# A routed mixture-of-experts kernel: the last sum of h ahead of the next expert's weight sums, and a buffer of its own for the odd group's outputs

## The chip, the cores and the metric

The kernel runs on one core of one Trainium2 chip. The metric is device time in microseconds of one execution, lower is better. Before the change three executions took 673.17, 674.33 and 680.16 us; the median is 674.33.

## What is computed

Two blocks follow each other. The first is attention within chunks of 64 tokens, for 8 batches, 8 heads and 576 tokens each. Its output, 4608 tokens by 512 channels, goes through a router with eight experts: each token takes the expert whose embedding is nearest by cosine, is sent through that expert's two weight matrices with a ReLU between, and is scaled by its gate. All is float32.

```python
logits = xn @ en.T / tau
expert_idx = np.argmax(logits, axis=1)
probs = np.exp(logits - logits.max(-1, keepdims=True)); probs /= probs.sum(-1, keepdims=True) + 1e-09
gate_w = probs[np.arange(N), expert_idx]
for e in range(E):                       # E = 8, N = 4608, D = 512, F = 1024
    mask = expert_idx == e
    h = np.maximum(x[mask] @ w1[e], 0.0)
    out[mask] = gate_w[mask, None] * (h @ w2[e])
```

## The kernel before

**The two halves.** In the first half, up to about 190 us, the kernel computes attention and the routing, and writes every token to a place in a table in DRAM that is sorted by expert. In the second half it takes the tokens in groups. A group is two lanes of 64 tokens, and each lane has its own expert: lane 0 starts at the first expert and goes up, lane 1 starts at the last and goes down. So a lane changes its expert now and then, while the other goes on with its own. Which groups change is known only at run time; the flags lie in a tile `swap`.

**A step.** The main loop over `j` computes the hidden layer of group `j + 1` in `hidden_fast`, then the second product of group `j` in `result`. Both are matmuls on TensorE (PE), at L342 and L413. `hidden_fast` saves multiplications in the manner of Strassen and Winograd: `x @ w1` is made of seven products of half-sized blocks, named p1 to p7 in the code. They are issued in the order p1, p2, p3, p5, p6, p7, p4. Some of them use blocks of `w1` itself (B11, B21, B22), the others sums of blocks: T1, T2 and T4 lie in the tile `sums`, T3 lies in the place of B12 within `w1`. The sums are made on VectorE (DVE) by `add_up` (L291). They depend on the expert alone, so they are made again only when a lane changes its expert.

Each of the seven products goes to a PSUM bank. Six banks rotate (`bank`), so a product must wait until the product issued six before it has been read. p4 waits for p1 of the same group, which is read by a copy on ScalarE (ACT, L377). p7 waits for p4 of the group before, which is read by the last sum of h.

**From products to h.** DVE adds the products into four quarters of h (L374: c11, c12, c22 and, last, U minus p4). After each quarter ACT applies the ReLU (L361, two instructions of 64 rows). When both quarters of a half of h are there, `turn` transposes that half on DVE (L368): `turn(0)` for the first, `turn(1)` for the second. The result `hT` is what L413 of the next step multiplies with `w2`.

**Around it.** `turn_next` transposes the inputs of the group after (L203), makes the sums of its inputs (L318, tile S) and issues further loads on the queue of SyncE (SP). The gate of that group is worked out a bit at a time between these (L224 to L234; its square root and its exponential each need a table load on ACT). `swap_next` calls `take_next` (L295 on): for each lane it loads the flag from `swap` into a register on DVE and on GpSimd (POOL), and branches. Only if the lane changes its expert, POOL copies three blocks of the new weights from `next_w1` over the old ones (L301), and DVE runs the four sums of `add_up`.

**The order.** The kernel gives the order by hand: each engine runs its instructions in the order of the code, and waits for others through semaphores. So what stands where in `hidden_fast` decides what is queued behind what on DVE and ACT.

**The outputs.** `result` scales the second product by the gate on ACT (L421) into a buffer `y`, of which there is one, and POOL scatters its rows to the output (L428). The group numbered `LEAST` may be a single lane (one lane has an odd group left over); then its outputs are 128 rows of 256, and it is handled in `step_alone` at the end, right behind `result` of the last pair (`before_last`).

Of the kernel before, what the change touches and what calls it, by code (L numbers as in the profile page):

```python
# [9 lines left out]
FP32 = mybir.dt.float32  # L10
# [8 lines left out]
P = 128  # L19
# [6 lines left out]
def kernel(  # L26
# [12 lines left out]
    B, H, S, Dh = q.shape  # L39
    E, D = moe_expert_emb.shape  # L40
# [3 lines left out]
    KD = D // P  # L44
# [4 lines left out]
    Q = 32  # L49
# [13 lines left out]
    def buf_of(j):  # L63
        return 0 if j < LONE else (j - LONE + 1) % 2
# [54 lines left out]
    bp = ctx.enter_context(tc.tile_pool(name="blk", bufs=2))  # L119
# [156 lines left out]
    def block(s, m, w1=None):  # L276

        if m in TS:
            return sums_sb[s][:, TS.index(m)]
        u, v = UV[m]  # L280
        return (w1 or w1_sb)[s].rearrange("p (u c) (v x) -> p u v c x", u=2, v=2)[:, u, v]
# [13 lines left out]
    def take_next(j):  # L295

        for s in range(2):
            f = number(swap[of_step(s, j)], 1, ENG.DVE, ENG.Pool)
            with tc.If(f > 0):  # L299
                for m in ("B11", "B21", "B22"):  # L300
                    nc.gpsimd.tensor_copy(block(s, m), block(s, m, next_w1))  # L301
                add_up(s, next_w1, ("T1", "T2", "T3", "T4"))

    def quarters(xT):
        return xT.rearrange("p (u c) (s b i) -> p u b c s i", u=2, s=2, b=2)
# [17 lines left out]
    def bank(ps_h, shape):  # L323
        tag = f"h{bank_no[0] % 6}"
        bank_no[0] += 1
        return ps_h.tile(shape, FP32, tag=tag, name=tag)

    def hidden_fast(j, ps_h, gate, turn_next, swap_next):

        d = mo[j]  # L330
        x = quarters(d["xT"])
        s1, s2, s3, s4 = d["S"]
        W2 = KF * Q

        def product(a, m):
            ps = bank(ps_h, [P, W2])
            for c in range(KD // 2):
                for s in range(2):
                    w = block(s, m)[:, c].rearrange("p (r x) -> p r x", r=2)
                    for r in range(2):  # L340
                        t0 = G * s + Q * r
                        nc.tensor.matmul(  # L342
                            ps[t0 : t0 + Q],
                            lhsT=a[:, c, s],
                            rhs=w[:, r],
                            start=c == 0,
                            stop=c == KD // 2 - 1,
                        )
            return ps


        last = "_last" if j == LEAST - 1 else ""
        hT = bp.tile([P, KF, P], FP32, tag="hT" + last, name="hT", bufs=1 if last else 2)
        d["hT"] = hT
        C = late_p.tile([P, 4, W2], FP32, tag="C", name="C")
        U, c11, c12, c22 = (C[:, i] for i in range(4))
        h = [late_p.tile([P, 2, W2], FP32, tag=f"h{b}", name=f"h{b}") for b in range(2)]

        def relu(b, v, x):
            for s in range(2):  # L360
                nc.scalar.activation(  # L361
                    h[b][G * v : G * v + G, s].rearrange("p (k i) -> p k i", i=Q),
                    x[G * s : G * s + G].rearrange("p (i k) -> p k i", i=Q),
                    AF.Relu,
                )

        def turn(b):
            nc.vector.transpose(  # L368
                hT.rearrange("p k (s b i) -> p b s k i", b=2, i=Q)[:, b],
                h[b].rearrange("p s (k i) -> p s k i", i=Q),  # L370
            )

        def add(out, a, b, op=ALU.add):
            nc.vector.tensor_tensor(out, a, b, op)  # L374

        p1 = product(x[:, 0, 0], "B11")
        nc.scalar.copy(U, p1)  # L377
        next(gate, None)
        next(gate, None)
        p2 = product(x[:, 1, 0], "B21")  # L380
        add(c11, U, p2)
        next(gate, None)
        relu(0, 0, c11)
        turn_next()
        p3 = product(s4, "B22")
        p5 = product(s1, "T1")
        p6 = product(s2, "T2")
        add(U, U, p6)
        add(c12, U, p5)
        add(c12, c12, p3)  # L390
        relu(0, 1, c12)
        for _ in gate:
            pass
        p7 = product(s3, "T3")
        add(U, U, p7)
        add(c22, U, p5)
        relu(1, 1, c22)
        p4 = product(x[:, 1, 1], "T4")
        swap_next()
        add(U, U, p4, ALU.subtract)  # L400
        relu(1, 0, U)
        turn(0)
        turn(1)

    def result(j, ps_y):
        d = mo.pop(j)
        ps = ps_y.tile([P, D], FP32, tag="y", name="y_ps")
        one_group = j == LEAST
        w = D // 2 if one_group else D
        for c in range(KF):  # L410
            for r in range(P // Q):
                t0, s, d0 = (r % 2, 0, w * (r // 2)) if one_group else (r, r // 2, 0)
                nc.tensor.matmul(  # L413
                    ps[Q * r : Q * r + Q, 0:w],
                    lhsT=d["hT"][:, c, Q * t0 : Q * t0 + Q],
                    rhs=w2_sb[s][buf_of(j)][:, c, d0 : d0 + w],
                    start=(c == 0),
                    stop=(c == KF - 1),
                )
        y = bp.tile([P, D], FP32, tag="y", name="y", bufs=1)  # L420
        nc.scalar.activation(y[:, 0:w], ps[:, 0:w], AF.Copy, scale=gate_of.pop(j))  # L421
        to, at, bound = out, spot[:, j % SPOTS, TOK : TOK + 1].bitcast(I32), N - 1
        if one_group:

            at2 = bp.tile([P, 1], I32, tag="at2", name="at2")
            nc.vector.tensor_scalar(at2, at, 2.0, second, ALU.mult, ALU.add)
            to, at, bound = out.rearrange("n (s d) -> (n s) d", s=2), at2, 2 * N - 1
        ins = nc.gpsimd.indirect_dma_start(  # L428
            out=to,
            out_offset=bass.IndirectOffsetOnAxis(ap=at, axis=0),  # L430
            in_=y[:, 0:w],
            in_offset=None,
            bounds_check=bound,
            oob_is_err=False,
        )
        tc.declare_no_dep(ins.ins, group="rows", reason="blocks hold different tokens")
        tc.add_to_no_dep_group("rows", ins.ins)
# [8 lines left out]
    with (  # L446
# [590 lines left out]
        for t in range(-3, NT + 3):  # L1037
# [24 lines left out]
            if 0 <= t < NT:  # L1062
                values(t)
                b = (2 * t + 2) // NCB + 1
# [43 lines left out]
    late_p = ctx.enter_context(tc.tile_pool(name="late", bufs=1, reuse_waits="tile"))  # L1108
# [11 lines left out]
    with (  # L1120
# [18 lines left out]
        for j in range(LEAST - 1):  # L1139
            n = j + 2  # L1140

            def turn_next():
                if n < LEAST:
                    turn_xb(n)
                    if n + XBUF < NJ:
                        load_x(n + XBUF)
                    add_x(n)

            def swap_next():
                if NE <= n < LEAST:  # L1150
                    take_next(n)

            if j == 0:
                first_parts()
                add_up(0, None, TS)
                first_parts()
            elif j == 1:
                turn_next()
                add_up(1, None, TS)
                hidden_plain(2, w1_sb, lambda s: add_up(s, None, ("T3",)))  # L1160
            else:
                gate = gate_parts(n) if n < LEAST else iter(())
                hidden_fast(j + 1, ps_h, gate, turn_next, swap_next)

            result(j, ps_y)
            if NE <= next_of(j) < NJ:
                load_w2(next_of(j))
# [9 lines left out]
        def before_last():  # L1177
            result(LEAST - 1, ps_y)
            load_w2(LEAST + 1)

        def step_alone(j, between=None):
            turn_xb(j)
            if j + XBUF < NJ:
                load_x(j + XBUF)
            gates(j)
            hidden_plain(j, next_w1)
            if j + 1 < NJ:
                load_late(j + 1)
            if between is not None:
                between()  # L1190
            result(j, ps_y)
            if j + 2 < NJ:
                load_w2(j + 2)
# [51 lines left out]
```

## Time and profile before

| | |
|---|---|
| median of three executions | 674.33 us |
| the profiled execution | 673.4 us |
| its span, first to last instruction | 671.6 us |
| share of the span busy: PE / DVE / ACT / POOL | 93% / 63% / 64% / 26% |
| mean granted TensorE clock | 0.978 |
| DVE, sums of w1 for a new expert (L291, from `next_w1`) | 6 changes of 4 sums, 1.22 us each |
| DVE, sums of h (L374) | 231, 0.416 us each; idle before them 49.8 us |
| DVE, `turn` (L368) | 66, 0.708 us each |
| ACT, ReLU (L361) | 264, 0.678 us each; idle before them 101.8 us |
| ACT, y (L421) | 37, 0.682 us each |

A row gives the time an engine was at work on such instructions, and the idle time that came just before them. Idle time of an engine that isn't the bound costs nothing by itself. An arrow in brackets, as in `[1.54 <-DVE C L374]`, names what ended that idle time: the engine, the tile and the line. An engine name with a q (DVEq) is its sequencer, which handles register loads, branches and waits. `x16` is the number of instructions merged into one row; their time is from the first's start to the last's end.

### The profile page before, as it was taken

Reading aid. Unit: us, or ns where it says so; the run is one execution under the profiler, and the core shown is the slowest. Engines: PE = TensorE matmul, PEld = TensorE weight load, DVE = VectorE, ACT = ScalarE, POOL = GpSimd, SP = SyncE. Lnnn points to the kernel's source line nnn. Section 1 sums busy time; section 2 is a strip of 40 time slices with the busy share of each in tenths; the row PEclk is TensorE's granted clock in tenths of the full one; section 3 lists DMA queues with packets and bytes.
Section 4 is the critical chain, followed back from the end, with each engine's and each line's share of the span. In section 5 each row is a group of like instructions: output and inputs, shape, how many; then the busy total and the mean of one; then the engine's idle time right before and its main releaser. Section 6 shows DMA issues by size and latency. Waiting matters only on the chain. (4 is left out here: it accounts for less than half of the span.)

```text
span 671.6 us, 24878 instructions
## 1 busy us (share of the span) xinstructions
PE 626.3 (93%) x9744; PEld 343.6 (51%) x9744; DVE 425.9 (63%) x1140; ACT 427.7 (64%) x758; POOL 175.2 (26%) x255
## 2 busy tenths in 40 slices
PE   4988999999899979999999999988999999999993
PEld 3867888786343436555434444433444444444441
DVE  2858888886498535656576566768565667565430
ACT  4656677675225837674867877565877766867740
POOL 6648887843320101002110102202101020100101
PEclk9889899999899979999999999999999999999998
DMA  9898899989818711112787111776821114511101
GB/s 246 221 267 232 245 290 289 278 247 367 316 45 300 294 34 46 44 39 61 286 313 254 54 36 47 283 283 227 325 77 37 50 44 164 175 43 34 50 26 39
DMA packets 94687, 112.67 MB, mean 168 GB/s; under 512 B 52460, under 2 KB 72684, under 8 KB 94552
## 3 DMA queue, kind: packets, MB, share of 16 engines
q1 hardware_dynamic: 82824, 72.84, 34.0%
q0 software_dynamic: 11696, 38.04, 17.1%
q8 instruction: 81, 1.33, 0.8%
q14 instruction: 54, 0.44, 0.2%
q10 hardware_dynamic: 32, 0.02, 0.0%
HBM read 334.71 MB, written 22.69 MB: 532 GB/s over the span
## 5 line engine op out<-in xcount | busy, mean ns | idle before, releaser
L413 PE MATMUL y_ps<-w,hT 128*32 128x512 f32 (+1 forms) x2368 | 265.4, 591 | 3.6 <-DMA w<-in_moe_w_dram 3.6
L361 ACT ACTIVATE h<-C 64x256 f32<-64x256 f32 x264 | 179.0, 678 | 101.8 <-DVE C L374 99.4
L413 PEld LDWEIGHTS y_ps<-w,hT 128*32 128x32 f32 x2368 | 84.1, 111 | 160.0 <-issue 147.6
L428 POOL DMA_INDIRECT out_dram<-y,spot x36 | 35.1, 975 | 414.9 <-ACT y L421 238.7
L374 DVE TENSOR_TENSOR C<-C,h 128x256 f32<-128x256 f32 x231 | 96.1, 416 | 49.8 <-DVEq L299 39.2
L342 PE MATMUL h<-sums,xbT 128*32 128x256 f32 x1056 | 81.0, 380 | 5.0 <-DVEq L299 2.6
L342 PE MATMUL h<-w,S 128*32 128x256 f32 x1056 | 81.4, 379 | 3.2 <-DVE w L291 1.7
L342 PE MATMUL h<-w,xbT 128*32 128x256 f32 x1056 | 68.5, 379 | 0.0
L368 DVE STREAM_TRANSPOSE hT<-h 128x512 f32<-128x512 f32 x66 | 46.7, 708 | 28.2 <-ACT h L361 28.1
L227 DVE TENSOR_SCALAR rn<-rn 128x1 f32<-128x1 f32 x37 | 5.7, 153 | 82.3 <-ACT rn L224 82.3
L342 PEld LDWEIGHTS h<-w,xbT 128*32 128x32 f32 x1056 | 37.7, 110 | 34.1 <-issue 17.0
L342 PEld LDWEIGHTS h<-sums,xbT 128*32 128x32 f32 x1056 | 38.5, 110 | 28.8 <-ACT C L377 4.3
L342 PEld LDWEIGHTS h<-w,S 128*32 128x32 f32 x1056 | 39.1, 110 | 26.0 <-DVE C L374 2.0
L421 ACT ACTIVATE y<-y_ps,gate 128x512 f32<-128x512 f32 (+1 forms) x37 | 25.2, 682 | 37.5 <-issue 25.9
L813 POOL DMA_INDIRECT spots<-xr,dest x36 | 37.4, 1038 | 30.3 <-DVE dest L778 9.8
L203 DVE STREAM_TRANSPOSE xbT<-xin 128x256 f32<-128x256 f32 x73 | 44.5, 649 | 0.5 <-DVE hT L368 0.5
L224 ACT ACT_TABLE_LOAD x34 | 43.6, 1283 | 0.9 <-issue 0.4
L231 ACT ACT_TABLE_LOAD x34 | 43.6, 1283 | 0.6
L342 PE MATMUL h<-sums,S 128*32 128x256 f32 x528 | 40.9, 379 | 0.0
L695 ACT COPY xT<-tr 128x512 f32<-128x512 f32 x36 | 21.1, 585 | 29.9 <-PE tr L693 29.9
L585 POOL DMA_DIRECT2D kx<-in_k_dram x36 | 32.0, 891 | 19.1 <-PE tr L608 18.3
L585 POOL DMA_DIRECT2D qx<-in_q_dram x40 | 34.5, 866 | 0.3 <-PE tr L608 0.2
(202 smaller groups left out, 801.6 us busy)
## 6 DMA issues: line engine op xcount, KB each, us to landing
w<-in_moe_w_dram SPq DMA_DIRECT2D x74, 2048.0 KB
next_w<-in_moe_w_dram SPq DMA_DIRECT2D x67, 2048.0 KB
xin<-spots SPq DMA_DIRECT2D x158, 64.0 KB
qx<-in_q_dram POOLq DMA_DIRECT2D x32, 256.0 KB
v<-in_v_dram SPq DMA_DIRECT2D x56, 144.0 KB
kx<-in_k_dram POOLq DMA_DIRECT2D x28, 256.0 KB
spots<-blank SPq DMA_DIRECT2D x9, 144.0 KB
spot<-spots SPq DMA_DIRECT2D x80, 4.0 KB
```

Source lines behind the costliest of these rows:

```text
L203: nc.vector.transpose(xT[:, :, cols].rearrange("p c (b i) -> p b c i", i=Q), t[:, s * (D // 2) : (s + 1) * (D // 2)].rearrange("p (b i c) ...
L224: nc.scalar.activation(rn, spot[:, j % SPOTS, SQ : SQ + 1], AF.Sqrt)
L231: nc.scalar.activation(sh, sh, AF.Exp, accum_out=gate)
L342: nc.tensor.matmul(ps[t0 : t0 + Q], lhsT=a[:, c, s], rhs=w[:, r], start=c == 0, stop=c == KD // 2 - 1,)
L361: nc.scalar.activation(h[b][G * v : G * v + G, s].rearrange("p (k i) -> p k i", i=Q), x[G * s : G * s + G].rearrange("p (i k) -> p k i", i=Q),
L368: nc.vector.transpose(hT.rearrange("p k (s b i) -> p b s k i", b=2, i=Q)[:, b], h[b].rearrange("p s (k i) -> p s k i", i=Q),)
L374: nc.vector.tensor_tensor(out, a, b, op)
L413: nc.tensor.matmul(ps[Q * r : Q * r + Q, 0:w], lhsT=d["hT"][:, c, Q * t0 : Q * t0 + Q], rhs=w2_sb[s][buf_of(j)][:, c, d0 : d0 + w], start= ...
L421: nc.scalar.activation(y[:, 0:w], ps[:, 0:w], AF.Copy, scale=gate_of.pop(j))
L428: ins = nc.gpsimd.indirect_dma_start(out=to, out_offset=bass.IndirectOffsetOnAxis(ap=at, axis=0), in_=y[:, 0:w], in_offset=None, bounds_ch ...
L585: eng.dma_start(out=x[done : done + n], in_=src[b, :, s : s + n, :].rearrange("h p d -> p h d"),)
L813: ins = nc.gpsimd.indirect_dma_start(out=spots, out_offset=bass.IndirectOffsetOnAxis(ap=at, axis=0), in_=m, in_offset=None, bounds_check=S ...
```

## The change

There are two edits. In `hidden_fast` the call of `swap_next()` moves from ahead of the last sum of h to a place between `turn(0)` and `turn(1)`. So on DVE the last sum (U minus p4) and `turn(0)`, and on ACT the ReLU of that sum, are issued before the flags are loaded and, where an expert changes, before the four sums of the next w1. In `result` the odd group takes a buffer of the tile S (two of them, used for the sums of inputs in the main loop) in place of the common `y`.

```diff
@@ hidden_fast
         p4 = product(x[:, 1, 1], "T4")
-        swap_next()
         add(U, U, p4, ALU.subtract)
         relu(1, 0, U)
         turn(0)
+        swap_next()
         turn(1)
@@ result
-        y = bp.tile([P, D], FP32, tag="y", name="y", bufs=1)
+        if one_group:
+            S = late_p.tile([P, 3, KD // 2, 2, Q], FP32, tag="S", name="S", bufs=2)
+            y = S.rearrange("p a c b i -> p (a c b i)")
+        else:
+            y = bp.tile([P, D], FP32, tag="y", name="y", bufs=1)
         nc.scalar.activation(y[:, 0:w], ps[:, 0:w], AF.Copy, scale=gate_of.pop(j))
```

## The prediction

> **What bounds the kernel now.** I read the busy table first: TensorE (PE) is busy for 93% of the span, no other engine for more than 64%. So the end can only move if PE's idle time, or work after PE's last matmul, moves. The chain of waits does not help here: it runs back through POOL's own queue. Next I cut the routed half into steps, from the first matmul of one group's second product (`result`, L413) to the first of the next, and asked for the busy time in six of them.
>
> ```profile
> PE 626.3 (93%) x9744; PEld 343.6 (51%) x9744; DVE 425.9 (63%) x1140; ACT 427.7 (64%) x758; POOL 175.2 (26%) x255
> ```
>
> ```profile
> 401.55:414.45 12.90, 12.90 (x180) 5.72 (x176) 7.23 (x20) 9.46 (x15) 3.98 (x4) 1.00 0.14 43
> 414.45:427.37 12.92, 12.92 (x181) 5.72 (x177) 9.61 (x19) 6.53 (x10) 1.11 (x2) 1.00 0.45 149
> 307.72:322.31 14.59, 13.89 (x188) 7.60 (x186) 10.77 (x21) 6.96 (x11) 2.15 (x3) 1.00 0.43 145
> 335.22:349.90 14.68, 13.72 (x180) 5.72 (x176) 11.92 (x23) 8.07 (x14) 3.20 (x4) 1.00 0.80 297
> 427.37:443.56 16.19, 13.35 (x180) 5.58 (x176) 12.34 (x25) 8.80 (x14) 3.80 (x4) 1.00 0.88 331
> 456.47:472.21 15.74, 13.73 (x181) 5.72 (x177) 12.98 (x23) 8.09 (x14) 2.60 (x3) 1.00 0.73 264
> ```
>
> After the window come its length, then PE's busy time. An undisturbed step lasts 12.9 and PE never rests in it. Six steps hold a change of w1 (sums at 313.9, 341.2, 418.1, 435.2, 463.5 and 553.3; call them S1 to S6). S3 (second line) and S6 still last 12.9. S1, S2, S4 and S5 are the last four lines: 1.7, 1.8, 3.3 and 2.8 too long, **9.6 us in all**. That is what this part of the change can win. (The steps starting at 240.5 and before are lengthened by a w2 load, 3.60 us of PE idle; nothing here touches that.)
>
> The timeline of VectorE (DVE), ScalarE (ACT) and PE in S4 shows the cause:
>
> ```profile
> 432.79 0.86 DVE L374 TENSOR_TENSOR C<-C,h 128x256 f32<-128x256 f32 x2
> 435.16 1.23 DVE L291 TENSOR_TENSOR sums<-next_w 128x1024 f32<-128x1024 f32 x1 [1.52 <-DVEq L299]
> ...
> 439.84 0.41 DVE L374 TENSOR_TENSOR C<-C,h 128x256 f32<-128x256 f32 x1
> 440.17 0.70 DVE L368 STREAM_TRANSPOSE hT<-h 128x512 f32<-128x512 f32 x1
> ```
>
> ```profile
> 440.28 1.36 ACT L361 ACTIVATE h<-C 64x256 f32<-64x256 f32 x2 [4.88 <-DVE C L374]
> 441.67 0.69 ACT L421 ACTIVATE y<-y_ps,gate 128x512 f32<-128x512 f32 x1
> 442.26 0.36 ACT L377 COPY C<-h 128x256 f32<-128x256 f32 x1
> ```
>
> ```profile
> 440.30 1.07 PE L342 MATMUL h<-w,S 128*32 128x256 f32 x16 [1.54 <-DVE C L374]
> 442.67 1.07 PE L342 MATMUL h<-sums,xbT 128*32 128x256 f32 x16 [1.30 <-ACT C L377]
> ```
>
> The last sum of h (439.84) stands behind the four sums of w1; ACT idles 4.88 for it, and the y and the copy of the next group's p1 stand behind its ReLU. PE waits twice for a PSUM bank: until that last sum has read p4 (1.54), then until the copy has read p1 (1.30).
>
> **What the Trainium skill says.** "PSUM — Partial Sum Buffer" (Engine vs sequencer instructions): ScalarE, VectorE and GpSimd run strictly first in, first out. The trace agrees: y and copy follow the ReLU at once, though y's matmuls ended by 434.4. "GPSIMD Engine Reference" (Specifications): GpSimd shares its SBUF interfaces with VectorE. It agrees: beside POOL's weight copies (411.4 to 414.4) the add of S at L318 took 0.54, elsewhere 0.29. "DMA: Bandwidth & Descriptors" (Anatomy of one DMA) puts a fixed 2.0 us on a transfer, mostly the write's receipt. It agrees: the last full y was handed over by 659.48 and its buffer came free about 661.6, 2.1 later.
>
> **Part 1: the moved sums.** No instruction is added or removed. Per step the block moved on DVE is two register loads and branches (skipped if the expert stays) and, for a changed lane, four sums of 1.22. It moves behind one add (0.42) and `turn(0)` (0.70). POOL's part (three copies of 1.03) is in the same block, but nothing else of POOL lies between, and its copies start when p3 frees them, before DVE gets there. The block issues no DMA and no SP work lies between; the next w1 load, which waits for the sums' reading, starts under 1 us later, and a lane's next change is at least 45 us away.
>
> *How much later the sums start.* In S3 the last c22 add starts at 417.36 and the sums at 418.06, 0.70 later: register load and branch. After: the moved add waits for c22's end (417.84), `turn(0)` follows 0.33 later (440.17 after 439.84), and needs the ReLU of c12, which ends at 418.15. So `turn(0)` at 418.2, sums at 418.9: **0.84 later**.
>
> *What that may cost.* Lane 1's first product with T1 waits for the whole of lane 0's block: PE restarted in S2 and S5 only after lane 0's fourth sum. In S3 that block ended at 422.88 and PE loaded T1's weights at 423.70. 422.88 + 0.84 + 0.05 = 423.77, a stall of 0.07. So S3 and S6 lose about 0.1 each.
>
> *What it gives.* The last sum and its ReLU no longer wait for the w1 sums, so both bank waits end early. In S4 (lane 1, no block of lane 0 ahead) each sum is also ready before its product. I follow the start of the last c22 add, relative to the step's start: 2.9 in S3. Register load to `turn(1)` then takes 6.5 for lane 0 and 7.6 for lane 1; the chain from `turn(1)` to the next last c22 add, with the ReLU and gate no longer late, is 0.7 + 5.3 (562.62 to 567.92), so the next step's value is x + 12.5 − 12.9 or x + 13.6 − 12.9. In a quiet step it falls by 12.91 − 11.35: ACT repeats every 11.55 when it is behind (copies at 560.71 and 572.26), of which only the 0.20 idle before the last ReLU goes. It stops at 2.4 (2.9 beside POOL's copies).
> - S1: x = 4.2. T1 is ready before PE wants it; the copy of p1 is in time. No stall.
> - S2: from S1, 4.9, then 3.3, plus about 0.7 beside POOL: 4.1 instead of 5.3. The lane-0 block ends at 4.1 + 0.84 + 5.52 + 0.05 = 10.5 after the start; PE wants it at 9.25. Stall 1.25.
> - S4: from S3, 2.9 − 0.4, plus 0.5: 3.0 instead of 5.9. No stall: **3.3** won.
> - S5: back at 2.9; stall 0.1: **2.7** won.
>
> S1 and S2 belong together: until S1's stall PE's column groups run about 0.8 apart (matmuls of two products alternate, `result` lasts 7.83 instead of 7.05), and the stall that aligns them costs that too. So S1 and S2, 3.45 before, keep about 1.35: **2.1** won. Sum: 2.1 + 3.3 + 2.7 − 0.2 = **7.9**. Bounds: 9.6, and about 5 if S2 gains nothing and each lane-0 change stalls by 0.3.
>
> *What hides the rest.* In quiet steps the register loads (1.5) move under the last ReLU, which `turn(1)` waits for anyway; DVE is idle there. That cover is 1.4 to 1.5 long, and if it goes, `turn(1)` has until the next `result`.
>
> **Part 2: the odd group's outputs.** One buffer was shared:
>
> ```profile
> 661.68 0.47 ACT L421 ACTIVATE y<-y_ps,gate 128x256 f32<-128x256 f32 x1 [3.45 <-DMA out_dram<-y,spot]
> 662.43 0.99 POOL L428 DMA_INDIRECT out_dram<-y,at  x1 [2.95 <-ACTq L1199]
> ```
>
> PE's last matmul ends at 660.86, so the eviction can start 0.75 earlier, and the scatter with it. In a buffer of S, free for many steps, no new wait arises: in the built program this eviction waits for PE and DVE alone. But SP's last load issue ends at 662.86, and the span at 671.6. Whether those 8 us follow POOL or SP the page does not show: gain 0 to 0.8; I take **0.4**.
>
> **Sum.** 7.9 + 0.4 = 8.3. The profiled execution took 673.4, so 665.1. The median of the runs shown is 674.33, 0.9 higher: **666.0**. About 1% (6.7 us, so 667.6) is what can be told from no change.
>
> **Rivals.**
> *Lag stays (0.23).* ACT is busy 9.5 of 12.9 in a step; if DVE's chain behind the sums does not shorten, S2 and S5 keep their waits and pay 0.84 each, S3 and S6 0.1 each. S1 (1.7) and S4 (3.3) still win. 5.0 − 1.9 + 0.4 = 3.5: 670.8. Against it: DVE's rn sits idle 1.73 for ACT after each such ReLU, which goes.
> *Slower (0.05).* `turn(0)` stands ahead of the sums and waits for ACT. If the ReLU of c12 comes late (it ended only 0.05 before it would be wanted), the delay d grows from 0.84, and every lane-0 change pays: S2 and S5 d each, S3 and S6 d − 0.8. With S1 and S4's 5.0 and the 0.4, it decides from 2d + 2(d − 0.8) = 5.4, d = 1.75. At d = 2.5 the kernel takes 677.
> *It does nothing (0.04).* PE's waits are replaced by one for w2: those loads, 4.2 MB, land 14.4 after `result` ends (329.96 after 315.55) and are wanted 18.8 after it. 4.4 are left, so I exclude nearly all of this: 674.3. That the order is not what the text says is excluded: DVE's built order has the add and `turn(0)` ahead of the loads in every step.
>
> **Numbers.** Forecast 0.68: 663.5 to 668. The range adds most of the first rival: 663.2 to 670.2. Faster by over 1%: 0.68 (nearly all of the forecast, little else); slower by over 1%: 0.03; the rest 0.29.
>
> **What would show it.** Right: no idle of PE before L342 put down to ACT C L377 or DVE C L374; S4's step near 12.9; S3 and S6 at most 13.1; S2 about 14; ACT's idle before its ReLU down from 99.4; the last eviction within 0.1 of PE's end. Wrong: lane-0 steps of 13.5 or more in S3, S5 and S6 (the delay is larger than 0.84), or S4 still above 14.5 (the lag stays).

## The result, and the profile after

The change makes the kernel faster, by about what was forecast. Over 14 executions each the medians are 668.01 us after and 676.60 before, a ratio of 0.987 with a 95% interval of 0.9838 to 0.9902. That is 8.6 us less (6.6 to 11.0 by the interval); 8.3 had been forecast. 668.01 lies within 663.2 to 670.2, at the upper edge of the 663.5 to 668 to which the forecast gave most of its chance; it is 2.0 above the 666.0 because this time the kernel before itself had a median 2.3 higher than the 674.33 that the forecast started from.

The profiled execution after took 667.17, with a span of 665.4 (before: 673.4 and 671.6). From its page, the busy table's first entries and the groups that answer to those of before:

```profile
PE 624.7 (94%) x9744; PEld 390.1 (59%) x9744; DVE 427.0 (64%) x1140; ACT 430.3 (65%) x758; POOL 180.7 (27%) x255
...
L361 ACT ACTIVATE h<-C 64x256 f32<-64x256 f32 x264 | 178.9, 678 | 71.7 <-DVE C L374 68.9
...
L374 DVE TENSOR_TENSOR C<-C,h 128x256 f32<-128x256 f32 x231 | 96.0, 416 | 11.2 <-PE h L342 4.4
L342 PE MATMUL h<-sums,xbT 128*32 128x256 f32 x1056 | 96.1, 379 | 0.6 <-DVEq L299 0.6
...
L368 DVE STREAM_TRANSPOSE hT<-h 128x512 f32<-128x512 f32 x66 | 46.7, 708 | 55.0 <-ACT h L361 54.2
```

No engine runs more or fewer instructions. ACT's idle time ahead of the ReLU fell from 101.8 to 71.7, and DVE's idle time ahead of the sums of h from 49.8 to 11.2, while that ahead of `turn` rose from 28.2 to 55.0: most of it only changed its place. The column to read is PE's. In the whole routed half PE idles 0.6 us for `hidden_fast`, in one place, where it idled 8.2 before (3.2 ahead of `h<-w,S` and 5.0 ahead of `h<-sums,xbT`).

The six steps with a change of w1, in the windows of the trace after (length, PE's busy time, then PE's weight loads, DVE, ACT, POOL):

```profile
310.62:323.53 12.91, 12.91 (x184) 8.45 (x180) 11.59 (x23) 8.21 (x14) 2.87 (x3) 1.00 0.33 100
336.44:349.35 12.91, 12.91 (x184) 8.45 (x180) 12.11 (x27) 9.77 (x16) 4.65 (x4) 1.00 0.69 238
...
413.89:426.81 12.92, 12.92 (x184) 8.46 (x180) 12.19 (x26) 9.49 (x16) 2.71 (x3) 1.00 0.43 139
426.81:439.71 12.90, 12.90 (x183) 8.44 (x179) 11.59 (x23) 8.09 (x12) 3.40 (x4) 1.00 0.84 305
...
452.62:466.50 13.88, 13.32 (x183) 7.35 (x179) 13.22 (x27) 10.26 (x17) 5.92 (x4) 1.00 0.58 198
543.96:557.07 13.11, 13.11 (x182) 5.68 (x178) 12.45 (x27) 10.13 (x17) 1.14 (x1) 1.00 0.44 144
```

S1 to S4 are undisturbed. S5 keeps 0.97 and S6 has 0.20 that it did not have before.

DVE and ACT in S4, the step that was 3.28 too long. First DVE:

```profile
430.89 1.38 DVE L374 TENSOR_TENSOR C<-C,h 128x256 f32<-128x256 f32 x3
432.18 0.70 DVE L368 STREAM_TRANSPOSE hT<-h 128x512 f32<-128x512 f32 x1
433.75 1.22 DVE L291 TENSOR_TENSOR sums<-next_w 128x1024 f32<-128x1024 f32 x1 [0.87 <-DVEq L299]
```

Then ACT:

```profile
430.74 4.15 ACT L361 ACTIVATE h<-C 64x256 f32<-64x256 f32 x6 [3.64 <-DVE C L374]
434.91 0.69 ACT L425 ACTIVATE y<-y_ps,gate 128x512 f32<-128x512 f32 x1
435.50 0.36 ACT L377 COPY C<-h 128x256 f32<-128x256 f32 x1
```

The last sum of h is the third of the row at 430.89 and follows c22 at once. The six ReLU instructions of three quarters run in one row, and y and the copy of p1 come right behind, 8.7 after the step's start at 426.81; before, the copy came 14.9 after it (442.26 in a step from 427.37). So p7 and p4 of the step find their banks free.

The end, from ACT's and POOL's timelines after:

```profile
655.81 0.47 ACT L425 ACTIVATE S<-y_ps,gate 128x256 f32<-128x256 f32 x1 [2.72 <-PE y_ps L413]
```

```profile
656.55 1.00 POOL L432 DMA_INDIRECT out_dram<-S,at  x1 [2.22 <-ACTq L1203]
```

PE's last matmul ends at 655.76, so this eviction starts 0.05 after it (0.82 before) and waits for PE alone.

**Where the span's 6.2 us come from.** I measure from the end of one step's y product to another's, since the starts shift with the offset between PE's column groups. From the end of the sixth y product to PE's last matmul: 396.95 before (263.91 to 660.86), 389.33 after (266.43 to 655.76), so 7.62 less. From PE's last matmul to the span's end: 10.76 and 9.63, so 1.13 less. Up to the sixth y product, where no expert changes and so no sums are moved, this execution took 2.52 more; in the traces below that point lies anywhere from 259.5 to 271.6. 7.62 + 1.13 − 2.52 = 6.2. In the routed steps the two traces agree to a hundredth wherever nothing changes, so I judge theories there and use the times for the sum.

### The profile page after: what moved, and what is told of

Same layout as the page of the kernel before. It is cut to its first block, busy times and chain, and to the rows that moved or that the text cites. A ratio compares the mean times of both kernels' runs of the same rounds, so it can differ in the third digit from the quotient of the medians.

```text
span 665.4 us, 24841 instructions
## 1 busy us (share of the span) xinstructions
PE 624.7 (94%) x9744; PEld 390.1 (59%) x9744; DVE 427.0 (64%) x1140; ACT 430.3 (65%) x758; POOL 180.7 (27%) x255
## 5 line engine op out<-in xcount | busy, mean ns | idle before, releaser
L413 PE MATMUL y_ps<-w,hT 128*32 128x512 f32 (+1 forms) x2368 | 273.7, 589 | 0.0
L361 ACT ACTIVATE h<-C 64x256 f32<-64x256 f32 x264 | 178.9, 678 | 71.7 <-DVE C L374 68.9
L413 PEld LDWEIGHTS y_ps<-w,hT 128*32 128x32 f32 x2368 | 117.7, 111 | 129.7 <-issue 65.0
L374 DVE TENSOR_TENSOR C<-C,h 128x256 f32<-128x256 f32 x231 | 96.0, 416 | 11.2 <-PE h L342 4.4
L342 PE MATMUL h<-sums,xbT 128*32 128x256 f32 x1056 | 96.1, 379 | 0.6 <-DVEq L299 0.6
L342 PE MATMUL h<-w,S 128*32 128x256 f32 x1056 | 95.7, 379 | 0.0
L342 PE MATMUL h<-w,xbT 128*32 128x256 f32 x1056 | 76.5, 379 | 0.0
L342 PEld LDWEIGHTS h<-sums,xbT 128*32 128x32 f32 x1056 | 53.6, 110 | 18.5 <-DVEq L299 1.5
L342 PEld LDWEIGHTS h<-w,S 128*32 128x32 f32 x1056 | 53.8, 110 | 17.3
L342 PEld LDWEIGHTS h<-w,xbT 128*32 128x32 f32 x1056 | 48.2, 110 | 24.5 <-issue 4.1
L425 ACT ACTIVATE y<-y_ps,gate 128x512 f32<-128x512 f32 x36 | 24.8, 688 | 45.4 <-issue 38.7
L342 PE MATMUL h<-sums,S 128*32 128x256 f32 x528 | 47.9, 379 | 0.0
```

Source lines behind the costliest of these rows:

```text
L342: nc.tensor.matmul(ps[t0 : t0 + Q], lhsT=a[:, c, s], rhs=w[:, r], start=c == 0, stop=c == KD // 2 - 1,)
L361: nc.scalar.activation(h[b][G * v : G * v + G, s].rearrange("p (k i) -> p k i", i=Q), x[G * s : G * s + G].rearrange("p (i k) -> p k i", i=Q),
L413: nc.tensor.matmul(ps[Q * r : Q * r + Q, 0:w], lhsT=d["hT"][:, c, Q * t0 : Q * t0 + Q], rhs=w2_sb[s][buf_of(j)][:, c, d0 : d0 + w], start= ...
```

## The experiments

Each kernel's row gives its ratio to the kernel before, executed beside it, and from its trace the routed steps (sixth y product to PE's last matmul) and the six steps' excess over 12.91. Waits in other steps show in the routed column alone.

| kernel | ratio to before, 95% interval | routed | S1 | S2 | S3 | S4 | S5 | S6 |
|---|---|---|---|---|---|---|---|---|
| before | | 396.95 | 1.68 | 1.77 | 0 | 3.28 | 2.83 | 0 |
| after | 0.987 (0.9838 to 0.9902) | 389.33 | 0 | 0 | 0 | 0 | 0.97 | 0.20 |
| p1_only | 0.991 (0.9863 to 0.9956) | 389.19 | 0 | 0 | 0 | 0 | 0.82 | 0.20 |
| p2_only | 0.998 (0.9933 to 1.0024) | 397.34 | 1.54 | 2.22 | 0 | 3.31 | 2.87 | 0 |
| add_only | 0.988 (0.983 to 0.9919) | 389.45 | 0 | 0 | 0 | 0 | 1.24 | 0 |
| both_turns | 1.015 (1.011 to 1.0195) | 407.51 | 1.73 | 5.73 | 4.52 | 0.13 | 3.99 | 2.97 |
| after_again | 0.986 (0.9819 to 0.9907) | 389.61 | 0 | 0 | 1.16 | 0 | 0.51 | 0.18 |
| loads_first | 1.004 (1.0016 to 1.0055) | 395.34 | 0 | 1.26 | 0.78 | 0 | 2.23 | 0.42 |
| add_loads | 1.000 (0.9979 to 1.0019) | 395.22 | 0 | 0.65 | 0.47 | 0 | 0.89 | 0.14 |
| seven_banks | 1.001 (0.998 to 1.003) | 399.03 | 0.54 | 1.96 | 0 | 2.85 | 4.82 | 0 |
| no_copies | one execution | 388.16 | 0 | 0 | 0 | 0 | 0 | 0 |
| no_copies_add | one execution | 388.16 | 0 | 0 | 0 | 0 | 0 | 0 |

### Each edit by itself

p1_only has the moved sums alone, p2_only the odd group's own buffer alone. Against the kernel before (here and below, several calls are written on one line to save room), p1_only:

```diff
- swap_next()
  add(U, U, p4, ALU.subtract); relu(1, 0, U); turn(0)
+ swap_next()
  turn(1)
```

and p2_only:

```diff
+ if one_group:
+     S = late_p.tile([P, 3, KD // 2, 2, Q], FP32, tag="S", name="S", bufs=2)
+     y = S.rearrange("p a c b i -> p (a c b i)")
+ else:
      y = bp.tile([P, D], FP32, tag="y", name="y", bufs=1)
```

> Only the moved sums; the odd group shares y as before. Theory (the last sum of h queued behind the w1 sums held two PSUM banks): the steps S1, S2 and S4 last 12.9, S5 about 13.9, S6 about 13.1, as in the changed kernel; 7.6 us of the 674 come from here, ratio 0.989. Rival (the odd group's buffer carries a good part): 0.992 or more, with the same steps.

> Only the odd group's own buffer; the sums stand where they stood. Theory: the last eviction starts within 0.1 us of PE's end in place of 0.8, and the time from PE's last matmul to the end of the span falls from 10.7 to about 9.6 to 10; ratio 0.998 to 0.999; S1, S2, S4 and S5 keep 1.7, 1.8, 3.3 and 2.8 of excess. Rival (the end follows SP, not POOL): the eviction moves and the time to the end stays 10.7; ratio 1.000.

The moved sums carry the result: p1_only takes 389.19 in the routed steps, as after. Its ratio alone would not decide, as the interval holds the values of both theories. p2_only keeps every stall; its traced execution was the longest of its six (680.77), but the extra time lies ahead of the routed steps, which begin at 271.65 in it. Here are PE's two waits in its S4, the same two as in the kernel before:

```profile
448.38 1.07 PE L342 MATMUL h<-w,S 128*32 128x256 f32 x16 [1.54 <-DVE C L374]
450.75 1.07 PE L342 MATMUL h<-sums,xbT 128*32 128x256 f32 x16 [1.30 <-ACT C L377]
```

The second edit does what it says. ACT's last eviction in p1_only, whose buffer is shared, and then in p2_only:

```profile
656.93 0.47 ACT L421 ACTIVATE y<-y_ps,gate 128x256 f32<-128x256 f32 x1 [5.13 <-PEq L1199]
```

```profile
669.08 0.47 ACT L425 ACTIVATE S<-y_ps,gate 128x256 f32<-128x256 f32 x1 [2.72 <-PE y_ps L413]
```

PE had ended at 654.47 in p1_only, 2.46 before the eviction, and at 668.98 in p2_only, 0.09 before it. p1_only's wait is longer than the 0.82 of before because the scatter that holds the buffer ended at 653.04 and the eviction's semaphore came at 656.85, 3.8 later; before, it was 2.1. What that is worth at the end is not resolved. From PE's last matmul to the span's end it is 9.6 to 10.7 in nine traces with the own buffer (mean 10.0) and 9.7, 10.8 and 11.5 in three with the shared one (mean 10.7). The ratio of p2_only, −0.7% to +0.2%, holds both the forecast's 0.4 us and nothing.

### Which of the moved instructions matters

add_only keeps both turns behind the sums and moves the add and its ReLU alone. both_turns moves `turn(1)` ahead of the sums as well. Against the kernel after, add_only:

```diff
  add(U, U, p4, ALU.subtract); relu(1, 0, U)
- turn(0); swap_next(); turn(1)
+ swap_next(); turn(0); turn(1)
```

and both_turns:

```diff
  add(U, U, p4, ALU.subtract); relu(1, 0, U)
- turn(0); swap_next(); turn(1)
+ turn(0); turn(1); swap_next()
```

> The last sum and its ReLU ahead of the w1 sums, both turns behind them; odd group's buffer as changed. Theory: the two bank waits hang on the last sum alone, so they are gone here too; the w1 sums start 0.3 to 0.4 earlier than in the changed kernel, so S6 loses its 0.2 and S5 some of its 1.0; turn(0) now follows the sums, 0.7 more on DVE ahead of the next gate. Ratio 0.986 to 0.988. Rival (turning the first half early carries the gain, as DVE's chain after the sums is what makes the next step late): S4, 13 us after S3, is too long again by 1 us or more, ratio 0.990 or above.

> Both turns ahead of the w1 sums. turn(1) waits for the ReLU of the last sum, which ends about 3.5 us after the last c22 add starts, so the w1 sums start 2.7 us later than in the changed kernel. Theory (PE wants lane 0's block, or lane 1's T1, 9.25 after the step's start, and every further delay is paid): each of the six changes stalls PE by about 2.5 to 3 us, 15 us more than the changed kernel; ratio to before 1.005 to 1.012. Rival (later sums are absorbed by a DVE that is idle a third of the time): 0.990 or below.

add_only does as well as the change: the gain comes from the add and its ReLU, and `turn(0)` ahead of the sums adds nothing to it. It even costs a little: in five of the six steps the sums start 0.2 to 0.4 later with it (S3: 4.58 after the step's start, and 4.16 here), and S6's 0.20 is gone here. S5, which was to get shorter too, got longer (1.24); its cause is below.

both_turns shows how near the order is to losing. DVE in its S3, and then PE:

```profile
431.35 0.71 DVE L368 STREAM_TRANSPOSE hT<-h 128x512 f32<-128x512 f32 x1 [2.02 <-ACT h L361]
432.05 1.23 DVE L291 TENSOR_TENSOR sums<-next_w 128x1024 f32<-128x1024 f32 x1
```

```profile
436.92 1.49 PE L342 MATMUL h<-sums,xbT 128*32 128x256 f32 x10 [2.69 <-DVEq L299]
```

DVE idles 2.02 at `turn(1)` until the last ReLU is done, and the sums wait behind it: they start 7.88 after the step's start. PE then waits for T1 in every change of lane 0 (2.1 to 2.9 in one wait); in the two changes of lane 1 the excess is 1.73 and 0.13. That is the forecast's slower rival (sums held behind a turn that waits for ACT), reached with one line more: the routed steps take 18.2 us more than after, where about 15 were expected.

### The banks alone

Does the loss in S4 come from the PSUM banks, as the forecast read it? seven_banks is the kernel before with seven banks in rotation for h and one, in place of two, for y.

```diff
- tag = f"h{bank_no[0] % 6}"
+ tag = f"h{bank_no[0] % 7}"
...
- tc.tile_pool(name="ps_y", bufs=2, space=PSUM, reuse_waits="tile") as ps_y,
+ tc.tile_pool(name="ps_y", bufs=1, space=PSUM, reuse_waits="tile") as ps_y,
```

> The kernel before with seven PSUM banks for the products of h and one for y in place of six and two; nothing else is moved. Theory (two of the waits were for banks): p7 no longer waits for the last sum of the group before, p4 waits for it in its place and no longer for ACT's copy of p1. S1 has no excess; S4 about 0.9 to 1.3 in place of 3.3; S2 and S5 keep 1.6 to 2.6, since there PE waits for lane 0's block of w1 sums; the routed steps gain 3.5 to 5 of the 9.6. Rival (the loss is the late ReLU, y and hT, not the banks): S1 and S4 keep 1.5 and 3 us.

PE's rows that waited in its S4 and S5:

```profile
435.63 1.07 PE L342 MATMUL h<-sums,xbT 128*32 128x256 f32 x16 [0.41 <-DVE C L374]
437.74 7.10 PE L413 MATMUL y_ps<-w,hT 128*32 128x512 f32 x64 [1.04 <-ACT y L421]
...
463.73 1.50 PE L342 MATMUL h<-sums,xbT 128*32 128x256 f32 x10 [2.87 <-DVEq L299]
```

The two waits of S4 for banks of h are down from 2.84 to 0.41, so they were bank waits. But y stands behind the late ReLU on ACT, and with one bank for it PE now waits there. The wait for T1 in S5 stays, as a bank can't help it; it is even longer (2.87, before 1.83), since the sums start 8.18 after the step's start there, before 7.03. As a whole the kernel gained nothing: the routed steps take 2.1 us more than before, where 3.5 to 5 less were expected, and S4 keeps 2.85 where 0.9 to 1.3 were expected. As a bank was taken from y at the same time, the run shows what the two waits were for, but not what a seventh bank alone would win. More banks treat one of two effects of the late sum; taking it out of the queue treats both.

### What is left in S5 and S6

after_again is the changed kernel once more.

> The changed kernel once more, beside the next three. Theory: S5 too long by 0.8 to 1.0, S6 by 0.2, all else 12.9; ratio 0.987. Rival (these leftovers are chance): S5 and S6 differ from that.

The gain repeats, but the leftovers move: S3 is 1.16 too long and S5 0.51. They follow one number, the end of lane 0's fourth sum of w1 counted from the step's start:

| step | the sums end at | less 9.74 | excess |
|---|---|---|---|
| after, S3 | 9.34 | −0.40 | 0 |
| after, S5 | 10.71 | 0.97 | 0.97 |
| after, S6 | 9.94 | 0.20 | 0.20 |
| p1_only, S5 | 10.56 | 0.82 | 0.82 |
| add_only, S5 | 10.98 | 1.24 | 1.24 |
| add_only, S6 | 9.65 | −0.09 | 0 |
| after_again, S3 | 10.90 | 1.16 | 1.16 |
| after_again, S5 | 10.25 | 0.51 | 0.51 |

(9.74 is read from S6 of after; the other rows test it. S2, S3 and S6 of the two kernels that come next, loads_first and add_loads, follow it too, with ends of 9.88 to 11.00. In both_turns S6 follows it, but S2, S3 and S5 are 1.6 to 1.7 longer than it says, and why is open.) So the question is what makes the sums end late. In S5 after, POOL, DVE and PE:

```profile
455.99 4.00 POOL L301 COPY w<-next_w 128x1024 f32<-128x1024 f32 x3 [6.03 <-DMA next_w<-in_moe_w_dram]
```

```profile
457.35 1.74 DVE L291 TENSOR_TENSOR sums<-next_w 128x1024 f32<-128x1024 f32 x1
459.12 1.94 DVE L291 TENSOR_TENSOR sums<-next_w,sums 128x1024 f32<-128x1024 f32 x1
```

```profile
463.44 0.84 PE L342 MATMUL h<-sums,xbT 128*32 128x256 f32 x10 [0.56 <-DVEq L299]
```

POOL's copies run late, beside the sums. The sums take 1.74 and 1.94 in place of 1.22, and the three copies 4.00 in place of 3.0. The trace puts POOL's 6.03 of idle time down to the load of `next_w`, which SP issued at 455.78, 0.2 before. The same 0.20 to 0.23 lies between this issue and the copies in S5 of p1_only, add_only, after_again, loads_first and add_loads, and in S2 of after (337.81 and 338.01). 2 MB in that time would be some 10,000 GB/s, and the busiest slice of the page of after shows 363; so the copies follow the issue itself, not the landing of new weights. The first attempt was therefore to have SP issue that load ahead of w2's, in the kernel after (loads_first) and in add_only (add_loads):

```diff
+ if NE - 1 <= n < LEAST - 1:
+     load_behind(n)
+ elif n == LEAST - 1:
+     load_late(LEAST)
  if NE <= next_of(j) < NJ:
      load_w2(next_of(j))
- if NE - 1 <= n < LEAST - 1:
-     load_behind(n)
- elif n == LEAST - 1:
-     load_late(LEAST)
```

> The changed kernel with the next w1 load issued on SP ahead of the next w2 load. Theory (in S5 POOL's copies waited for SP to reach the next_w1 load of the step before, 455.99 after an issue at 455.78; they then ran beside DVE's first sums, which took 1.74 and 1.94 in place of 1.22): SP reaches it about 2.9 us earlier, the copies start by 453.5 on the same scale, the sums take 1.22 again, S5's excess falls from 1.0 to 0.2 or less. 0.8 us or 0.1% in all. Rival (the copies are late for another reason, for example p3 not yet read): copies and S5 as before, S5's excess 0.8 to 1.0. A second way to lose: SP now waits ahead of the w2 load for the sums to have read next_w1, w2 comes 2 us later, and result waits for it.

> As the last, and both turns behind the w1 sums (only the last sum and its ReLU ahead). Theory (each lane-0 change has only 0.8 us of room, and turn(0) ahead takes 0.34 of it): S6's 0.2 goes as well, every step lasts 12.9 but for 0.1; the routed steps from the 5th to the end take 388.0 to 388.4 us against 389.3 in the changed kernel; ratio 0.985 to 0.987. Rival (turn(0) behind the sums makes the next step late): an excess in S4 of 0.5 or more.

It failed. SP in loads_first is held in a small load ahead of it, and PE now waits for w2:

```profile
447.83 4.10 SPq L159 DMA_DIRECT2D spot<-spots  x1
...
457.66 1.37 SPq L177 DMA_DIRECT2D next_w<-in_moe_w_dram  x2
```

```profile
457.48 6.63 PE L413 MATMUL y_ps<-w,hT 128*32 128x512 f32 x58 [2.01 <-DMA w<-in_moe_w_dram]
```

The load is issued at 457.66 and the copies start at 457.89, 3.45 after the step's start (3.36 in the kernel after): no earlier. The routed steps take 6.0 more than after, with waits for w2 of 2.01 and 1.67 among them and later sums in S2 and S3 (they end at 11.00 and 10.52), so the gain is lost again. The sums are late because the copies of S2 came earlier there, 0.75 ahead of the step's start as in the kernel before, and two of DVE's sums of inputs took 1.01 each beside them, in place of 0.29; in S3 it is the 128x8 row shown below, with 1.79. add_loads has its copies in S5 earlier, at 2.25, and its sums end at 9.86; it pays for w2 too (0.66 and 2.74).

The second attempt leaves the copies out, to see what they cost DVE; its output is therefore not the reference's.

```diff
- for m in ("B11", "B21", "B22"):
-     nc.gpsimd.tensor_copy(block(s, m), block(s, m, next_w1))
  add_up(s, next_w1, ("T1", "T2", "T3", "T4"))
```

> The changed kernel without POOL's three copies of the new weights per change (L301), so a lane keeps the blocks B11, B21 and B22 of its first expert and the output is not the reference's; the four sums of w1 stay as they are. Theory (the copies lock DVE's operations with two SBUF inputs out): in the step of S5 the first two sums take 1.22 to 1.24 in place of 1.74 and 1.94, the 0.97 that this step is too long goes to 0.1 or less, S6's 0.20 goes to 0.1 or less, and S3 is not late; the routed steps take about 389.33 - 1.1 = 388.2 and every step 12.9. Rival (the leftover is the later start of the sums itself, 0.84 to 1.1): sums of 1.22 too, but S5 keeps 0.5 or more and S6 0.2. Second rival (DVE's slow sums have to do with the 4.19 MB of loads on SP's queue): the sums of S5 still take 1.7 or more.

> The kernel that moves the last sum and its ReLU alone ahead of the sums of w1 (both turns behind them, the odd group's own buffer), again without POOL's three copies, so a lane keeps the blocks B11, B21 and B22 of its first expert and the output is not the reference's. Theory (the copies lock DVE out): S5's two slow sums of 2.05 and 1.94 take 1.22 to 1.24, its 1.24 too long goes to 0.1 or less, and no other step is longer than 12.95; the routed steps take 389.45 - 1.24 = 388.2. Rival (lateness of DVE's own chain): S5 keeps 0.5 or more. Second rival (the loads): the sums of S5 still take 1.7 or more.

S5 in no_copies, DVE:

```profile
459.26 1.22 DVE L291 TENSOR_TENSOR sums<-next_w 128x1024 f32<-128x1024 f32 x1
460.52 1.23 DVE L291 TENSOR_TENSOR sums<-next_w,sums 128x1024 f32<-128x1024 f32 x1
```

Both kernels take 388.16 in the routed steps, where 388.2 was expected; PE waits for nothing in them. The sums of S5 end 8.98 after the step's start. So what the change leaves, 1.17 us, comes with POOL's copies, and neither with the moved sums' later start alone nor with the weight loads alone. (PE has to wait for the copies too, and these runs take that wait out as well. It shows once, 0.26 in S5 of add_only; in the table above the sums' end accounts for the excess of every step.)

How the copies get in DVE's way is also visible. From S3 of after_again, POOL and DVE:

```profile
410.14 3.01 POOL L301 COPY w<-next_w 128x1024 f32<-128x1024 f32 x3
```

```profile
411.40 1.79 DVE L229 TENSOR_SCALAR sh<-spot,lmax,rn 128x8 f32<-128x8 f32 x1
```

An operation on 128x8 that takes 0.29 elsewhere ends 0.03 after the last copy: it was held until POOL was done. The sums of S3 started 1.56 later than in the kernel after, where this row took 0.32, so 1.47 of it is this row. The Trainium skill, "SBUF — State Buffer" (Who interferes with whom), states the mechanism: VectorE and GpSimd share one pair of ports, an instruction locks it for its whole length, and the second to come waits fully; among VectorE's operations it names those with two inputs in SBUF against a GpSimd operation that reads SBUF, and `tensor_scalar` where it runs in a mode that uses both ports. The 128x8 operation is a `tensor_scalar`; in which mode it ran no run shows. For two inputs the trace agrees: in S5 after, the first sum of w1 ended 1.08 after the end of the second copy (459.09 and 458.01), the second sum 1.07 after that of the third (461.06 and 459.99). It agrees on what is spared, too: a sum of h (one input in PSUM) at 456.35 took 0.42 and `turn(0)` at 456.68 took 0.70 beside a copy, as always.

S6's 0.20 comes the same way. Its sums took 1.22 each, but they started 1.56 later than before (5.18 and 3.62 after the step's start), and 0.63 of this is the same 128x8 row, which took 0.53 in S6 before and here, beside the copies of 540.89 to 543.90:

```profile
541.78 1.16 DVE L229 TENSOR_SCALAR sh<-spot,lmax,rn 128x8 f32<-128x8 f32 x1
```

Left open: why SP is held in a small load (1.84 at 432.70 and 2.57 at 443.55 in the kernel after, 4.10 in loads_first, 0.52 in quiet steps). These fall together with the 4.19 MB of weights under way on the same queue; loading `spot` from another queue was not tried. Nor was a place for the copies where DVE has no such operation; it could win 1.2 us at most, a fifth of a per cent.

## Why the prediction was right, and where it was off

The sign, the cause and the size hold. By its steps:

- **What can be won, 9.6.** Mis-sized by 0.8. Counted by the ends of the y products it is 8.8: S1's stall of 1.68 at the starts costs only 0.90 at the ends, because it also brings PE's column groups back into line. The forecast knew of that effect, but booked it as a loss within S1 and S2, not as less to win.
- **S4, 3.3 won.** Right: 3.28, and both bank waits are gone. The way there had a miss that cost nothing: the last c22 add started at 4.52, not 3.0, as two sums of inputs took 1.01 each beside the copies; in a change of lane 1 PE has the room for it.
- **S1 and S2, 2.1 won with 1.25 of stall left in S2.** Too little: all of it went, 2.7 by the ends. Two terms were off. "Plus about 0.7 beside POOL" assumed the copies at their old place, just ahead of the step; they came 1.58 after its start, behind DVE's input sums, so the last c22 add started at 2.99, not 4.1, and the sums of w1 ended at 9.30, not 10.4. That was luck: a late issue on SP held the copies back, and in loads_first, where they came at the old place, S2 kept 1.26. The other term is the limit. A weight load at 9.25, seen once in S3 of before, stands for a last sum that ends at 9.14 (0.06 more to the block's end, 0.05 to the load); in the steps above the limit is 9.74. Of the 1.35 that S1 and S2 were to keep, 0.1 isn't worked out.
- **S5, 2.7 won with 0.1 left.** Too much: 1.86 won, 0.97 left. The last sum ended at 10.71 in place of the 9.20 that the forecast's terms give (2.9 + 0.84 + 5.52, less the 0.06 from the last sum to the block's end). Of these 1.51, 1.24 lie in the two sums that POOL's copies held up, and 0.30 in a last c22 add at 3.20 instead of 2.9. By the forecast's own limit this would have cost 1.57, so the limit, wrong the other way, hid a part of the miss. The forecast placed the copies ahead of DVE's block ("its copies start when p3 frees them, before DVE gets there"); in S5 a load issued late on SP, not p3, released them. It had also read the effect of POOL beside DVE as some tenths per operation, where an operation can be held for up to two copies. The trace it started from showed this: in S5 of before the 128x8 row at 456.11 took 2.08 beside the copies.
- **Sums 0.84 later.** About right in S3: 3.61 before and 4.58 after, so 0.97. Not in S6, where it is 1.56, 0.63 of it from the held 128x8 row.
- **S3 and S6 lose 0.1 each.** Right in sum: 0 and 0.20. The limit of 9.74 saved S3, whose sums ended at 9.34. Without the copies neither loses anything, so S6's 0.20 is again the copies'. In after_again, the same kernel, S3 lost 1.16.
- **Part 1, 7.9.** 7.62 measured: 2.68 + 3.28 + 1.86 − 0.20. The two errors, +0.6 in S1 and S2 and −0.8 in S5, nearly cancel, so the sum is better than its parts.
- **Part 2, 0.4.** The eviction moved as said (0.82 to 0.05 after PE's end); its worth at the end is not resolved. The 2.0 us that the forecast took from the Trainium skill, "DMA: Bandwidth & Descriptors" (Anatomy of one DMA), for a transfer's fixed cost fitted the kernel before (2.1); p1_only shows 3.8, so what a shared buffer costs here varies, 0.82 in one trace and 2.46 in the other.
- **The rivals.** "Lag stays" asked for S2 and S5 to keep their waits; S2 kept nothing. "Slower" needed the ReLU late for `turn(0)`; it was not, and both_turns shows that loss with `turn(1)`. Of the signs of being right, S2 at about 14 did not come (12.91). Of the signs of being wrong, one did in part: a lane-0 step of 13.5 or more, in S5 (13.88), and in after_again in S3 (14.07). It was to show that the delay is larger than 0.84; what it showed was the copies.

## What to carry to other kernels

On an engine that runs in order, look at what is queued behind a long block that only some steps contain: a short last step of the current work (here one add of 0.42 us) that frees a bank and feeds another engine belongs ahead of a long preparation of the next, but an instruction that itself waits for a slow neighbour does not. When a transfer or a helper engine's copies are said to be "out of the way", check in each affected step what releases them, since a lock or a queue can put them beside the very work that now has no slack. And measure by steps between like points: the routed steps repeat to a few tenths here, while whole executions differ by several us.

## What the runs showed of the hardware

- DVE and POOL took turns by whole instructions: sums of w1 of 1.22 took 1.37 to 2.05 beside copies, sums of inputs of 0.29 up to 1.16, one 128x8 operation 0.29 to 2.08 by where in the copies it fell, and a copy of 1.03 took 2.03 when a sum held it. With three copies back to back DVE could miss its turn at the end of one or two of them (the 1.79 spans the end of the second; the 2.08 of before, at 456.11, spans the ends at 456.20 and 457.17).
- A scatter's buffer came free 2.1 to 3.8 us after the scatter's own row ended.
- An issue of a 4 KB load on SP took 0.5 us in quiet steps, and up to 4.1 (loads_first) while 4.19 MB of weights were under way on its queue.
